# Strips of 64 bytes between the tiles of x, and one tile less for inner results, in a fused attention and expert kernel

## The chip, the core and the metric

The kernel runs on one core of a Trainium2 chip. The metric is the device time of one execution in microseconds (us). The time before is the median of 2 runs; the profile is of one more execution.

## The reference

Three stages follow each other. N is 2,304 tokens, D is 512.

```python
# 1 attention with keys and values averaged over 8 positions
k_p, v_p = k.reshape(B, H, 72, 8, 64).mean(3), v.reshape(B, H, 72, 8, 64).mean(3)
x = softmax(q @ k_p.T / 8) @ v_p                # 4 x 8 heads, 576 queries, 64 wide
x = x.transpose(0, 2, 1, 3).reshape(2304, 512)
# 2 a dense layer
h = x @ w_in                                    # 512 -> 2048
x = (h * cos(h)) @ w_out                        # 2048 -> 512
# 3 eight experts, weighed by a gate that is normalized eight times over rows and columns
P = exp(x @ w_gate - max); 8 times: P /= rowsum; P /= colsum; P *= N / E
out = sum over e of P[:, e] * (relu(x @ w1[e]) @ w2[e])   # 512 -> 1024 -> 512
```

## The kernel before, in words

**Arithmetic.** Every large product is made from numbers that are split into a high and a low part (float32r). Of the four partial products three are made: high by high, high by low, low by high. So each block of 128 by 128 weights costs three matmuls.

**Experts.** An expert's 1,024 inner columns are cut into two units of 512, so there are 16 units. The tokens are cut into three pairs of blocks, each block 384 tokens wide. A *step* is one unit with one pair; there are 48. A step has a first layer and a second layer, both in a scheme of seven products (P1, P5, P6, P2, P7, P3, P4, in this order) instead of eight. The first layer (`first_layer`, matmuls at L1178) makes the seven products for each half h of the unit: 2 x 7 products of 6 matmuls, 384 columns each, 84 in all. Its moving operand is a tile of x (`xc`), its weights are `whi` and `wlo`. It writes the PSUM tiles px, py and pv. ACT and DVE turn the results into 14 pairs of inner tiles `gh`, `gl`. The second layer (`strassen_layer`, matmuls at L1563) takes them as weights and streams `vhi` and `vlo`, 256 columns each, into the PSUM tiles pc and qc: 126 matmuls a step. While one step's second layer runs, the first layer of the next step runs between its parts.

**Tiles in SBUF.** The pool `xp` has eight tiles of 6,144 bytes a partition. In the attention and the dense layer they are x itself (`xh`, `xl`) and other things; in the experts seven of them hold the seven forms of x, one fixed tile for each product, and the eighth is `spare`, which DVE and ACT use. Each of the seven is filled again by a DMA from DRAM (`x_loaded`, issued by SP) for every step. Right behind the pool `xp` lies the pool `wp`: 14 tiles of 2,048 bytes for `whi` and `wlo`. 6,144 is three times 2,048, so before the change all these tiles start at the same remainder modulo 2,048 bytes (704). Within a tile the kernel reads pieces that start at multiples of 512 bytes. The inner tiles are 1,536 bytes; their pools hold 6 + 12 for `gh` and 6 + 12 for `gl` (GB = 12).

**Order.** Nothing is issued in the order of the Python code. Every operation becomes a node of a graph with an engine and a duration that the code states. `Graph.schedule` simulates five engines, and takes again and again the operation that can start first (of those near it the one with the earliest due time). It gives out the tiles too: an operation whose kind has no free tile can't be taken. This makes the order that each engine has on the chip. Where the simulated PE would idle by over 0.5 us it puts in filler matmuls (`keep_busy`, L529). The order of the pool tiles in memory is that in which they are first used: xh1, xh2, xl1, xl3, xl2, xh3, xh0, xl0.

Of the kernel before, what the change touches and what calls it, by code (L numbers as in the profile page):

```python
# [10 lines left out]
F32 = mybir.dt.float32  # L11
# [12 lines left out]
P = 128  # L24
# [41 lines left out]
class Slot:  # L66

    def __init__(self, group, pool, tag):
        self.group, self.pool, self.tag, self.free, self.holder, self.kinds = group, pool, tag, 0.0, None, []


class Group:

    def __init__(self, graph, name, side, after=(), over=None):
        self.graph, self.name, self.side, self.after, self.over = graph, name, side, after, over
        self.kinds, self.pools, self.stack, self.users, self.closed = [], {}, None, 0, False

    def ready(self):
        return self.stack is not None or (
            all(g.users == 0 for g in self.after) and (self.over is None or self.over.ready()))  # L80
# [72 lines left out]
class Graph:  # L153
# [119 lines left out]
    def schedule(self, log=None):  # L273
# [28 lines left out]
        while left:  # L302
# [38 lines left out]
            for buf in node.bufs:  # L341
                kind = buf.kind
                if not kind or buf.slot:
                    continue
                kind.queue.remove(buf)
                slot = slots.pop(0)
                slot.group.open()
                slot.holder, buf.slot = buf, slot
                buf.tile = slot.group.pools[slot.pool].tile(buf.shape, buf.dtype, tag=f"{slot.pool}{slot.tag}", name=buf.name)
            gap = start - free[e] + (0.6 if 19.0 < start < 27.0 else 0.0)  # L350
            if e == "PE" and self.fill and gap > 0.5:
                room = last and last.spare and all(
# [96 lines left out]
def fused_kernel(ctx: ExitStack, tc: tile.TileContext, qT, kT, kS, vS, v0, k1, v1, wa1, wb1, wa2, wb2, wg, out):  # L449
    nc = tc.nc  # L450
    g = Graph(ctx, tc)
    add, buf = g.add, g.buf

    W1, W2, GB, XR, T5 = 14, 14, 12, 7, 2
    base = g.group("base")
    first = g.group("first")
# [6 lines left out]
    more = g.group("more", "left", (second,))  # L463
# [6 lines left out]
    def many(group, pool_name, n, strict=False):  # L470
        return g.kind(group, pool_name, [str(i) for i in range(n)], strict)
# [30 lines left out]
    k_s5, k_c22, k_t5 = many(late, "cps", 2), many(late, "cpc", 1), many(late, "cpt", T5)  # L502
    k_acc2 = {2 * pair + j: k for pair, ks in ((1, [many(more, f"acx{n}", 1, True) for n in range(2)]), (0, k_acc[2:]),
                                               (2, k_acc[:2])) for j, k in enumerate(ks)}
    k_gbh, k_gbl = (g.join(many(first, a, 6), many(more, b, GB), strict=3) for a, b in (("gph", "gbh"), ("gpl", "gbl")))

    def banks(*names, strict=False):
        return g.kind(psum, "ps", [str(n) for n in names], strict)
# [1186 lines left out]
```

## Time and profile before

| | us |
|---|---|
| median of 2 runs | 1903.39 (1903.32 to 1903.47) |
| profiled execution | 1907.59 |
| its span, first to last instruction | 1905.9 |
| PE busy in it | 1889.6 (99%) |
| DVE, ACT, POOL busy | 1504.0, 1102.6, 360.7 |
| last 48 steps (experts), from first to last matmul | about 500 to 1901 of the span |

The profiled execution is 4.2 us (0.2%) above the median of the runs. PE is the matmul engine; its weight loads have a row of their own, PEld. A matmul's own duration overlaps the next one, since matmuls are pipelined. What a matmul costs is therefore the distance from its start to the next start; the chain of waits shows it, because it counts each stretch once.

### The profile page before, as it was taken

To read this page: it belongs to the slowest core of one execution; us is meant where nothing else is said; L and a number is where in the kernel's file an instruction comes from. 1 tells how busy PE (TensorE), PEld (TensorE's weight loads), DVE (VectorE), ACT (ScalarE), POOL (GpSimd) and SP (SyncE) were. 2 spreads that over 40 slices of the span, in tenths; PEclk is the share of its full clock that TensorE was granted. 3 is DMA by queue.
4 is the path that set the end of the run, shared out by engine and by line. 5 is a ranking of instruction groups with operands and counts; after the bars stand their busy time and mean duration, and the time that the engine had idled before them with its cause. 6 is when DMAs were issued, how large, how long until landed. Compare 5 with 4: busy or idle time off the path is not lost.

```text
span 1905.9 us, 33965 instructions
## 1 busy us (share of the span) xinstructions
PE 1889.6 (99%) x13032; PEld 1853.0 (97%) x13032; DVE 1504.0 (79%) x2721; ACT 1102.6 (58%) x2375; POOL 360.7 (19%) x260
## 2 busy tenths in 40 slices
PE   9999999999999999999999999999999999999999
PEld 7789998899999999999999999999999999999998
DVE  7998856987787787778787787877877877878776
ACT  5865434675566665555555565555555565655653
POOL 0213332242102021212122121212121120212120
PEclk9999999999999999999999999999999999999999
DMA  8856662577656556556456465565465564655653
GB/s 267 245 187 238 239 169 71 188 256 263 232 224 254 202 202 262 187 210 243 185 208 257 155 250 212 191 261 198 196 243 194 199 265 160 244 221 191 235 217 116
DMA packets 104762, 406.76 MB, mean 213 GB/s; under 512 B 11160, under 2 KB 15896, under 8 KB 102552
## 3 DMA queue, kind: packets, MB, share of 16 engines
q1 hardware_dynamic: 102616, 400.01, 56.2%
q0 software_dynamic: 1984, 4.59, 1.4%
q8 instruction: 102, 1.67, 0.3%
q14 instruction: 60, 0.49, 0.1%
HBM read 363.40 MB, written 41.16 MB: 212 GB/s over the span
## 4 chain that ended last, share of the span: by engine, by line
PE 93%; DVE 4%; ACT 2%; DMA 1%; issue 0%; SPq 0%; ACTq 0%; DVEq 0%
PE pc L1563 20%; PE py L1178 17%; PE qc L1563 16%; PE px L1178 11%; PE pv L1178 11%; PE po L989 3%; PE po L990 3%; PE po L991 3%; PE ph L989 2%; PE ph L990 2%; PE ph L991 2%; PE px L897 1%; PE ptr L883 0%; DMA wc<-wac 0%; DVE xd L557 0%
## 5 line engine op out<-in xcount | busy, mean ns | idle before, releaser
L1563 PE MATMUL pc<-vlo,gh 128*128 128x256 f32 x1152 | 318.0, 276 | 0.0
L1563 PE MATMUL pc<-vhi,gl 128*128 128x256 f32 x1152 | 318.0, 276 | 0.0
L1563 PE MATMUL pc<-vhi,gh 128*128 128x256 f32 x1152 | 318.0, 276 | 0.0
L1178 PE MATMUL py<-xc,whi 128*128 128x384 f32 x1152 | 293.7, 335 | 0.0
L557 DVE TENSOR_TENSOR gl<-sf,gh 128x384 fp32r<-128x384 f32 x384 | 228.4, 624 | 29.4 <-ACT gh L540 29.2
L540 ACT ACTIVATE gh<-sf 128x384 fp32r<-128x384 f32 x384 | 194.8, 524 | 93.6 <-DVE sf L557 91.5
L1563 PE MATMUL qc<-vhi,gh 128*128 128x256 f32 x864 | 241.7, 280 | 0.9 <-DVE qc L557 0.5
L1563 PE MATMUL qc<-vlo,gh 128*128 128x256 f32 x864 | 239.0, 277 | 0.0
L1563 PE MATMUL qc<-vhi,gl 128*128 128x256 f32 x864 | 238.9, 276 | 0.0
L557 POOL TENSOR_TENSOR raw<-raw 128x512 f32<-128x512 f32 x46 | 60.1, 1307 | 930.3 <-DVE wlo L557 584.4
L1563 PEld LDWEIGHTS pc<-vhi,gh 128*128 128x128 f32 x1152 | 216.3, 188 | 0.1
L1563 PEld LDWEIGHTS pc<-vhi,gl 128*128 128x128 f32 x1152 | 216.3, 188 | 0.0
L1563 PEld LDWEIGHTS pc<-vlo,gh 128*128 128x128 f32 x1152 | 216.2, 188 | 0.0
L1178 PEld LDWEIGHTS py<-xc,whi 128*128 128x128 f32 x1152 | 199.3, 188 | 0.9 <-ACT py L540 0.6
L1178 PE MATMUL px<-xc,whi 128*128 128x384 f32 x768 | 196.5, 336 | 0.0
L1178 PE MATMUL pv<-xc,whi 128*128 128x384 f32 x768 | 196.1, 336 | 0.0
L1178 PE MATMUL py<-xc,wlo 128*128 128x384 f32 x576 | 192.5, 334 | 0.0
L1563 PEld LDWEIGHTS qc<-vhi,gh 128*128 128x128 f32 x864 | 162.1, 188 | 4.6 <-DVE qc L557 0.9
L1563 PEld LDWEIGHTS qc<-vhi,gl 128*128 128x128 f32 x864 | 162.4, 188 | 0.0
L1563 PEld LDWEIGHTS qc<-vlo,gh 128*128 128x128 f32 x864 | 162.1, 188 | 0.0
L1178 PEld LDWEIGHTS px<-xc,whi 128*128 128x128 f32 x768 | 130.1, 188 | 0.6 <-issue 0.6
L1178 PEld LDWEIGHTS pv<-xc,whi 128*128 128x128 f32 x768 | 130.3, 188 | 0.0
(245 smaller groups left out, 4578.6 us busy)
## 6 DMA issues: line engine op xcount, KB each, us to landing
xc<-xc SPq DMA_DIRECT2D x357, 768.0 KB, 6.7
wc<-wac SPq DMA_DIRECT2D x112, 256.0 KB, 4.6
raw<-wb SPq DMA_DIRECT2D x32, 512.0 KB, 7.8
raw<-wa SPq DMA_DIRECT2D x32, 512.0 KB, 4.7
raw<-wa SPq DMA_DIRECT2D x8, 1024.0 KB, 7.2
raw<-wb SPq DMA_DIRECT2D x8, 1024.0 KB, 6.2
wac<-m SPq DMA_DIRECT2D x12, 512.0 KB, 6.3
wac<-cw SPq DMA_DIRECT2D x12, 512.0 KB, 3.7
```

The costliest lines, as they stand in the source:

```text
L540: lambda: nc.scalar.activation(out=out(), in_=in_(), func=func, **{k: v() if callable(v) else v for k, v in more.items()}),
L557: (nc.gpsimd if e == "G" else nc.vector).tensor_tensor(out=out(), in0=in0(), in1=in1(), op=op)
L897: nc.tensor.matmul(out=bank[e * D:(e + 1) * D, off:off + n], lhsT=vs[b][:, 2 * hp + e, :], rhs=pt[:, 2 * hh + e, off:off + n], start=(off ...
L989: nc.tensor.matmul(out=ps, lhsT=lh, rhs=rh, start=(i == 0), stop=False)
L990: nc.tensor.matmul(out=ps, lhsT=lh, rhs=rl, start=False, stop=False)
L991: nc.tensor.matmul(out=ps, lhsT=ll, rhs=rh, start=False, stop=(i == total - 1))
L1178: nc.tensor.matmul(out=ps(), lhsT=l[:, k], rhs=r[:, c, :], start=(start and c + n == 0), stop=(c + n == 3), skip_group_check=True)
L1563: nc.tensor.matmul(out=ps, lhsT=l[:, r], rhs=m[:, k], start=(start and h + n == 0), stop=(h + n == 3), skip_group_check=True)
```

## The change

Three things are done. A strip of 64 bytes is taken from the pool `xp` before each of its tiles, in order of first use, but not before the fourth (`spare`'s neighbour); one more strip follows the eighth. That is eight strips, 512 bytes. To have room, the second part of the pool for `gl` has 11 tiles instead of 12.

```diff
         self.kinds, self.pools, self.stack, self.users, self.closed = [], {}, None, 0, False
+        self.seen = []
...
                 slot.holder, buf.slot = buf, slot
+                if slot.pool == "xp" and slot not in slot.group.seen:
+                    slot.group.seen.append(slot)
+                    n = len(slot.group.seen)
+                    if n != 4:
+                        slot.group.pools[slot.pool].tile([P, 16], F32, tag=f"xpgap{n}", name="gap")
                 buf.tile = slot.group.pools[slot.pool].tile(buf.shape, buf.dtype, ...)
+                if slot.pool == "xp" and len(slot.group.seen) == 8:
+                    slot.group.seen.append(None)
+                    slot.group.pools[slot.pool].tile([P, 16], F32, tag="xpgap9", name="gap")
...
-    k_gbh, k_gbl = (g.join(many(first, a, 6), many(more, b, GB), strict=3) for a, b in (("gph", "gbh"), ("gpl", "gbl")))
+    k_gbh, k_gbl = (g.join(many(first, a, 6), many(more, b, n), strict=3) for a, b, n in (("gph", "gbh", GB), ("gpl", "gbl", GB - 1)))
```

Where the tiles start, as the two programs lay them out (remainder modulo 2,048 bytes):

| tile (product in the experts) | before | after | x minus weights, modulo 512, before | after |
|---|---|---|---|---|
| xh1 (P7) | 704 | 768 | 0 | 64 |
| xh2 (P1) | 704 | 832 | 0 | 128 |
| xl1 (P2) | 704 | 896 | 0 | 192 |
| xl3 (`spare`) | 704 | 896 | 0 | 192 |
| xl2 (P3) | 704 | 960 | 0 | 256 |
| xh3 (P4) | 704 | 1024 | 0 | 320 |
| xh0 (P5) | 704 | 1088 | 0 | 384 |
| xl0 (P6) | 704 | 1152 | 0 | 448 |
| weights `whi`, `wlo` | 704 | 1216 | | |

The second layer's tiles keep their distances: `gh` and `gl` start at 448 modulo 512 before and after, `vhi` and `vlo` at 128, so the moving operand minus the weights is 192 in both.

The instruction counts stay, but for two filler matmuls. PE's order is the same up to the first expert unit; from there a few places of it move, since the pool of `gl` is smaller. In the steady state it repeats every three steps; one of three is as before.

The first place is the 25th step on PE. py is P6 of the first half, px is P2; pc is the second layer. Before:

```order
L1178 MATMUL py<-xc,whi 128x384 x2
L1178 MATMUL py<-xc,wlo 128x384
L1178 MATMUL py<-xc,whi 128x384 x2
L1178 MATMUL py<-xc,wlo 128x384
L1563 MATMUL pc<-vhi,gh 128x256
L1563 MATMUL pc<-vlo,gh 128x256
L1563 MATMUL pc<-vhi,gl 128x256
```

Changed (the lines stand nine further down):

```order
L1187 MATMUL py<-xc,whi 128x384 x2
L1187 MATMUL py<-xc,wlo 128x384
L1187 MATMUL py<-xc,whi 128x384 x2
L1187 MATMUL py<-xc,wlo 128x384
L1187 MATMUL px_14292<-xc,whi 128x384 x2
L1187 MATMUL px_14292<-xc,wlo 128x384
L1187 MATMUL px_14292<-xc,whi 128x384 x2
L1187 MATMUL px_14292<-xc,wlo 128x384
L1572 MATMUL pc<-vhi,gh 128x256
```

P2 moved ahead of 12 matmuls of the second layer. This is so in one of three steps.

The second place is SP's queue in the same stretch; xc is a tile of x, raw a tile for weights of the second layer (wb) or the first (wa). Before:

```order
L562 DMA raw_13175<-wb 128x1024
L562 DMA xc<-xc 128x1536
L562 DMA raw_13199<-wb 128x1024
L562 DMA raw<-wa 128x1024
L562 DMA xc<-xc 128x1536 x7
```

Changed:

```order
L571 DMA xc<-xc 128x1536 x14
L571 DMA raw_13191<-wb 128x1024
L571 DMA raw_13205<-wb 128x1024
L571 DMA raw<-wa 128x1024
L571 DMA xc<-xc 128x1536 x7
```

The first load of wb now stands behind a load of x that was behind it.

The third place is PE at the end of the last step's first layer, where py is P4 of the second half. Changed:

```order
L1187 MATMUL py<-xc,whi 128x384 x2
L1187 MATMUL py<-xc,wlo 128x384
L1187 MATMUL py<-xc,whi 128x384 x2
L1187 MATMUL py<-xc,wlo 128x384
L538 MATMUL pc<-ident 128x128 x2
```

The last row, two filler matmuls, is new.

## Rows read from the trace of the kernel before

**Rows 1.** The page: engines, busy us, share of the span, instructions.
```profile
PE 1889.6 (99%) x13032; PEld 1853.0 (97%) x13032; DVE 1504.0 (79%) x2721; ACT 1102.6 (58%) x2375; POOL 360.7 (19%) x260
```

**Rows 2.** Windows: stretch, length, each engine's busy us, granted clock, DMA share.
```profile
600.00:1880.00 1280.00, 1280.00 (x9265) 1277.01 (x9265) 1003.26 (x1832) 735.34 (x1634) 222.09 (x159) 1.00 0.56 215
```

**Rows 3.** Chain of waits, 600 to 1880: shares of the stretch by line.
```profile
by line: PE pc L1563 28.2%; PE py L1178 21.6%; PE qc L1563 21.4%; PE px L1178 14.5%; PE pv L1178 14.4%
```

**Rows 4.** Windows of one line alone, L1178 then L1563 (PE, PEld busy and counts).
```profile
600.00:1880.00 1280.00, 710.28 (x3709) 627.58 (x3709) 1.00 0.56 215
...
600.00:1880.00 1280.00, 698.84 (x5556) 684.50 (x5556) 1.00 0.56 215
```

**Rows 5.** Chain of waits, 918 to 947, in order: start, us, what.
```profile
919.08 1.05 PE py L1178 x6
920.12 1.36 PE pc L1563 x12
921.49 1.04 PE px L1178 x6
922.53 1.04 PE py L1178 x6
923.57 0.68 PE qc L1563 x6
...
924.93 1.05 PE pv L1178 x6
```

**Rows 6.** Chain of waits, 420 to 445 (the dense layer).
```profile
422.03 1.04 PE pv L1178 x6
423.07 1.04 PE py L1178 x6
424.12 0.18 PE po L989
...
424.66 1.04 PE px L1178 x6
425.70 1.04 PE pv L1178 x6
```

**Rows 7.** Timeline, weight loads then matmuls: start, us, engine, line, operation.
```profile
602.58 0.36 PEld L1178 LDWEIGHTS px<-xc,whi 128*128 128x128 f32 x2
...
602.58 0.33 PE L1178 MATMUL px<-xc,wlo 128*128 128x384 f32 x1
```

**Rows 8.** Timeline: a `gl` tile is written, an older one's last read, its first read.
```profile
1237.53 0.55 DVE L557 TENSOR_TENSOR gl<-spare,gh 128x384 fp32r<-128x384 f32 x1
...
1239.43 0.28 PE L1563 MATMUL pc<-vhi,gl 128*128 128x256 f32 x1
...
1252.28 0.28 PE L1563 MATMUL pc<-vhi,gl 128*128 128x256 f32 x1
```

**Rows 9.** Timeline of SP, then the matmul that reads the first of these tiles.
```profile
1183.83 3.77 SPq L562 DMA_DIRECT2D xc<-xc  x3
1187.65 0.57 SPq L562 DMA_DIRECT2D raw<-wb  x1
1189.69 0.32 SPq L562 DMA_DIRECT2D xc<-xc  x1
1190.85 0.33 SPq L562 DMA_DIRECT2D raw<-wb  x1
...
1194.66 0.52 PE L1178 MATMUL px<-xc,whi 128*128 128x384 f32 x2
```

**Rows 10.** Loads of x, 600 to 1880, issue to landing.
```profile
DMA to landing us min/median/max: 4.0/6.8/9.2
```

**Rows 11.** Timeline of ACT: the first read of a loaded wb tile.
```profile
1212.24 0.64 ACT L540 ACTIVATE vhi<-raw 128x512 fp32r<-128x512 f32 x1
```

**Rows 12.** Filler matmuls of L529 by tile: count, duration ns min/median/max.
```profile
L529 PE MATMUL px<-ident x10: 275/275/377, 25.0 to 27.1; 128*128 128x128 f32 x10
```

## The prediction

> **What bounds the kernel now.** I began with the shares of the engines: PE is busy for 99% of the span [rows 1]. Then the windows, since an average hides stages: in the experts, from 600 to 1880 us, PE is busy in all 1280.00 us at a granted clock of 1.00, while DVE has 277 us to spare (1003 of 1280), ACT 545 and POOL over 1000 [rows 2]. The granted clock of 1.00 is the upper of the two levels, 2.4 GHz. So in two thirds of the kernel nothing counts but what a matmul costs and whether PE is made to wait.
>
> What a matmul costs is read from the chain of waits, stretch by stretch [rows 5]: six matmuls of the first layer take 1.04 us, so 173.3 ns each; twelve of the second take 1.36 us, six 0.68, so 113.3 ns. Now the average: the first layer's three tiles have 14.5 + 21.6 + 14.4 = 50.5% of the stretch [rows 3], which is 646.4 us for 3709 matmuls [rows 4], 174.3 ns each. The second layer's 49.6% are 634.9 us for 5556, 114.3 ns each. Both layers stand 1 ns above their floor. In the whole stretch that is 3.6 us in the first layer and 5.4 us in the second. All waits and all disturbance of PE are in these 9 us; the reader should keep this number, since a change that only takes disturbance away can't give more.
>
> **The strips.** They move the moving operand of the first layer against its weights. Do the two disturb each other at distance 0? They are read at the same time: the load of the next weights starts with the matmul, both at 602.58 [rows 7]. But the rows show no harm in it. First, the floor is reached at distance 0: px and py at 921.49 and 922.53 take 1.04 us [rows 5], and there all pieces are a multiple of 512 bytes apart. Second, in the dense layer the products of the same kind take the same 1.04 us [rows 6]; the four in these rows stream other tiles of x past other weights, by the layout at 64, 64, 256 and 320. The second layer of the experts, at 192, keeps to one floor throughout, too. Third, the excess shows where it comes from: a product takes 1.05 us where it follows the second layer (py at 919.08, pv at 924.93) and 1.04 where it follows another product. It is a change from 256 to 384 columns, some 0.01 us each, not a matter of seven tiles that all lie alike. Something like it stands in the dense layer, where three matmuls of po take 0.18 instead of 0.17 each behind py [rows 6].
>
> So the bounds of the strips are: a gain of 3.6 x 4032 / 3709 = 3.9 us if all excess of the first layer were a clash, and a loss from distances that no row shows. Of the seven, 64, 192, 256, 320 and 448 have been seen (448 in the last matmul of the second layer, while `whi` is loaded); 128 and 384 haven't. Those are P1 and P5: 2 products x 2 halves x 6 matmuls x 48 steps = 1152. The worst that a row shows for one matmul of this width beside its floor is 0.18 against 0.1733, 6.7 ns: 1152 x 6.7 ns = 7.7 us. I take 0, the value of five distances out of seven.
>
> The Trainium skill, page "SBUF — State Buffer", section "Who interferes with whom", gives PE two independent read ports, one for the moving operand and one for the weights, and says that PE never waits on anyone. By that rule the strips are worth exactly 0; the trace agrees as far as it goes.
>
> `spare` moves too, and the tiles of x in the dense layer. DVE and ACT have the slack named above, and in the dense layer PE could win no more than the same nanosecond for each of some 1,100 matmuls, so I put both at 0.
>
> **One tile less for `gl`.** A step needs 14; there were 18, now there are 17. What is hit is a `gl` that is written while 17 others are held. In the experts that is one of 14 writes in a step; reckoned buffer by buffer it is always one that is early. The example: DVE writes it at 1237.53; the oldest of the others is last read at 1239.43 and so is free at 1239.71; PE first reads the new one at 1252.28 [rows 8]. Written 2.2 us later it would still be 12 us early. The other two kinds of step have 3.1 and 6.2 us to wait with 15 and 18 us of room. So the tile itself costs 0; what can cost is the order that follows from it.
>
> **The order on PE.** In two of three steps a few products move by two to five groups of six matmuls of the second layer. The number of changes from second to first layer stays (424 before, 422 after), so that excess stays too. I counted the distance on PE between each product and the next that needs its result, with 1.04 us a product and 0.68 a group. The tightest of each kind stays as it was: P1 to P6 1.72 us, P6 to P7 2.40, P4 to the next P6 2.76. One shrinks, P7 to P4 of the first half, from 5.12 to 3.76 us; but 3.76 is what the second half has in every step, without a wait. Cost 0.
>
> P2 of the first half moves 1.36 us ahead in one step of three, and its tile is loaded again for each step. The load is issued at 1183.83, the matmul starts at 1194.66 [rows 9]: 10.83 us, the least that any of the seven has. Loads of x take 6.8 us, 9.2 at most [rows 10]. With 1.36 us less there are 9.47 us: still above 9.2. Cost 0, with the thinnest cover of all that I found.
>
> **SP's queue.** The first wb load moves behind a load of x that waits for PE: from 1187.65 to behind 1189.69, some 2.4 us. Its first reader is at 1212.24 [rows 11], 24 us after the old issue. Cost 0.
>
> **The end.** Two filler matmuls before the last stretch of the second layer. Each stands in the trace as two records; with 275 ns as the duration of one [rows 12] 4 x 0.275 = 1.1 us is the upper bound, and since durations overlap I take half, 0.5 us. The planner puts them where it saw PE wait anyway.
>
> **The sum.** 0 + 0 + 0 + 0.5: the profiled execution would take 1908 instead of 1907.59. It stands 4.2 us above the median of the runs; against the median that makes 1903.9, so 1904. About 2% (38 us) is what a measurement of this kernel can tell from no change, and this is far inside.
>
> **Rivals.**
> 1. *The excess is a clash and the strips end it.* Against it: the three points above. For it: all tiles lay at distance 0 wherever 1.05 stands, so no row shows the same change of width at another distance. 1903.4 - 3.9 = 1899.5. Chance 0.15.
> 2. *The floor itself is a clash.* 384 columns at 2.4 GHz are 160 ns; the rows show 13.3 ns more. If the strips gave that back: 4032 x 13.3 = 54 us, 1850 us. Against it: the same floor at distances 64, 256 and 320, and a surplus that grows with the columns (6.7 ns at 256, 13.3 at 384) while the weight load beside it stays the same. Chance 0.01. The Trainium skill, page "TensorE: Matmul & The Clock Gate", section "Back-to-back issue gap", gives N / 2.4 + 2.5 ns; by that formula 384 columns cost 162.5 ns, and 4032 x 10.8 = 44 us would be open. The trace disagrees with it at every distance it has.
> 3. *The load for P2 comes too late (slower).* This decides from 9.47 us on. 16 steps have the earlier P2. If their loads land as late as the worst seen, 9.2, nothing happens; two wb loads of 512 KB that now follow each other could add a microsecond or two: 16 x 1.5 = 24 us, 1927. For 2% each of the 16 would have to be 2.4 us late. With rows of 6.8 us in the median: chance 0.06, of that 0.01 for over 2%.
> 4. *The unseen distances 128 and 384 clash.* 1903.4 + 7.7 = 1911. Chance 0.04.
> 5. *The change doesn't do what it says.* The layout does show the seven distances, so this is left at 0.
>
> The forecast, no change by more than 2 us: 0.74.
>
> **Range and chances.** Down to 1898, which holds rival 1 and a little for the dense layer; up to 1910, which holds most of rival 4 and the smaller outcomes of rival 3. Left out are the floor, late loads in earnest, and an offset between runs. Faster by over 2%: 0.01 (rival 2). Slower by over 2%: 0.01 (rival 3). Within: 0.98.
>
> **What would show it.** In the changed profile: px, py and pv still near 50.5% of the stretch from 600 to 1880. If 1.05 becomes 1.04 for products behind the second layer, rival 1 holds. If one product of P1 or P5 takes more than 1.05 while P7 doesn't, rival 4. Idle time of PE before px at L1187 that ends with a DMA is rival 3. The forecast is wrong if PE's busy share of the experts falls under 99%, or if the floors of 1.04 and 0.68 us move at all.

## The result, and the profile after

The changed kernel takes 1927.37 us (median of two runs, 1924.46 and 1930.27), the one before 1903.39. The ratio is 1.0122 (1.0102 to 1.0143). It is 24 us slower, where 1904 was forecast, with 1910 as the upper end.

First the page of the changed kernel, the line that answers to [rows 1].

```profile
PE 1907.7 (99%) x13036; PEld 1869.8 (97%) x13036; DVE 1502.6 (78%) x2723; ACT 1096.9 (57%) x2374; POOL 367.3 (19%) x259
```

PE's busy time has grown by 18.1 us with four matmul records more, while DVE, ACT and POOL stand within 7 us of where they stood. So PE does the same work more slowly. The same windows as in [rows 2] and [rows 4], first all engines, then the first layer's line alone, then the second layer's:

```profile
600.00:1880.00 1280.00, 1277.03 (x9141) 1272.57 (x9140) 988.55 (x1811) 724.66 (x1620) 231.43 (x160) 1.00 0.57 213
...
600.00:1880.00 1280.00, 705.52 (x3654) 618.85 (x3655) 1.00 0.57 213
...
600.00:1880.00 1280.00, 698.61 (x5487) 687.02 (x5485) 1.00 0.57 213
```

The granted clock is 1.00 as before (the upper level, 2.4 GHz), and yet PE gets through 9141 matmuls in these 1280 us instead of 9265: 1.3% fewer. For 3.0 us it isn't busy at all; before it always was. The busy time by line doesn't show which matmuls are slower, since matmuls overlap. The chain of waits does. The stretch that answers to [rows 5], in the 14th step (start, us, what):

```profile
918.53 0.68 PE qc L1572 x6
919.21 0.68 PE pc L1572 x6
919.89 0.68 PE qc L1572 x6
920.57 0.68 PE pc L1572 x6
921.25 1.05 PE py L1187 x6
922.30 0.71 PE qc L1572 x6
923.01 0.71 PE pc L1572 x6
923.72 0.71 PE qc L1572 x6
924.42 1.05 PE px L1187 x6
925.48 1.06 PE pv L1187 x6
926.54 0.69 PE qc L1572 x6
927.23 1.04 PE py L1187 x6
928.27 1.36 PE pc L1572 x12
929.63 1.04 PE px L1187 x6
930.68 1.05 PE py L1187 x6
931.72 0.71 PE qc L1572 x6
932.43 0.71 PE pc L1572 x6
933.14 1.04 PE pv L1187 x6
934.18 0.68 PE qc L1572 x6
```

This is the main finding, and it is to be read from top to bottom. In this stretch pv at 925.48 is P5 and px at 924.42 is P1. Six matmuls of the second layer take 0.68 us, four times in a row. Then one product of the first layer runs (py, P4, whose x now lies at 320 from the weights), and from then on the same six take 0.71, three times in a row. Behind P1 and P5 (128 and 384) it is 0.69, all but the fast form. P6 (py at 927.23, distance 448) is followed by the fast form (1.36 for twelve), P2 and P7 (929.63, 930.68; 192 and 64) by the slow one, P3 (933.14; 256) by the fast one again. The second layer's own tiles haven't moved against each other. It has two speeds; it changes from one to the other at products of the first layer, and then it mostly stays for the whole stretch.

Over all steps, worked out from every matmul's start in the trace, gaps of over 30 ns left out: the second layer's mean distance from start to start is 113.52 ns before and 115.77 after. Of its stretches from 600 us on, 5% were slow (above 115.8 ns) before and 49% are after. P3 is always followed by a fast stretch (89 of 89), P4 and P1 together always by a slow one (58 of 58). But the last product and its distance don't decide alone: P4 by itself is followed by a slow stretch in 23 of 30 cases, P5 and P6 together in 14 of 14 behind a fast stretch and in none of 31 behind a slow one. So what ran before counts as well.

The second piece is the idle time of PE. The list of waits of the changed kernel (600 to 1880 us; before, it was empty):

```profile
PE py L1187 <- DVE pv L566: 3.0, 14, 0.2
```

With this most of the 24 us are divided. In the profiled executions the experts last from the first matmul's start to the last's 1402.8 us before and 1421.7 after: +18.9. Second layer: 6,048 matmuls x 2.25 ns = 13.6 us. First layer: 4,032 x 0.48 ns (174.27 to 174.75) = 1.9 us. The gaps of over 30 ns: 6.6 to 9.7, so 3.1 us. That makes 18.6. The experts also begin 3.8 us later (498.6 to 502.4); in ten kernels with the old order on every engine they begin between 491.0 and 501.3, so I don't put this down to the change. The matmuls into `po` ahead of the experts, some 1,100, cost 173.82 ns before and 174.04 after, which is 0.2 us in all.

### The profile page after: what moved, and what is told of

The parts are those of the page before. It is cut to its first block, busy times and chain, and to the rows that moved or that the text cites. A ratio compares the mean times of both kernels' runs of the same rounds, so it can differ in the third digit from the quotient of the medians.

```text
span 1928.5 us, 33987 instructions
## 1 busy us (share of the span) xinstructions
PE 1907.7 (99%) x13036; PEld 1869.8 (97%) x13036; DVE 1502.6 (78%) x2723; ACT 1096.9 (57%) x2374; POOL 367.3 (19%) x259
## 4 chain that ended last, share of the span: by engine, by line
PE 85%; DVE 9%; DMA 2%; ACT 2%; issue 1%; SPq 0%; POOL 0%; DVEq 0%; POOLq 0%; ACTq 0%
PE pc L1572 19%; PE py L1187 15%; PE qc L1572 15%; PE pv L1187 10%; PE px L1187 9%; PE po L998 3%; PE po L999 3%; PE po L1000 3%; DVE gl L566 2%; PE ph L998 2%; PE ph L1000 2%; PE ph L999 2%; DVE sf L566 1%; DMA wsum<-wac 1%; DVE acc L1559 1%
## 5 line engine op out<-in xcount | busy, mean ns | idle before, releaser
L566 DVE TENSOR_TENSOR gl<-sf,gh 128x384 fp32r<-128x384 f32 x384 | 207.4, 569 | 31.4 <-ACT gh L549 31.3
```

Of the source, the lines that this page charges most:

```text
L566: (nc.gpsimd if e == "G" else nc.vector).tensor_tensor(out=out(), in0=in0(), in1=in1(), op=op)
```

## The experiments

Two theories stood at the start. **D**: the distance between the first layer's moving tile and its weights makes the loss. **O**: the moved order does. Later D was split into **X** (x minus the first layer's weights alone decides) and **G** (the places of all four groups of tiles against each other).

The table holds all kernels. W1 are the first layer's weights (`whi`, `wlo`), W2 the second's (`gh`, `gl`), v its moving tiles (`vhi`, `vlo`). The distances are in bytes modulo 256; that 256 is the period is shown below. "Second" and "first" are the mean ns from start to start, "experts" is from their first matmul to the last, in us. All three are of the profiled execution. The ratio is that of the runs, against the kernel before beside them.

| kernel | x-W1 | v-W2 | x-W2 | v-W1 | second | first | experts | ratio |
|---|---|---|---|---|---|---|---|---|
| before | 0 | 192 | 0 | 192 | 113.52 | 174.27 | 1402.8 | 1 |
| after | mixed | 192 | mixed | 192 | 115.77 | 174.75 | 1421.7 | 1.0122 |
| e1 | 0 | 192 | 0 | 192 | 113.47 | 174.27 | 1406.4 | 1.0011 |
| e4 (256) | 0 | 192 | 0 | 192 | 113.39 | 174.19 | 1405.4 | 1.0020 |
| e2 (64) | 64 | 192 | 64 | 192 | 117.81 | 173.43 | 1423.1 | 1.0111 |
| e3 (64) | 64 | 192 | 64 | 192 | 117.67 | 173.41 | 1426.8 | 1.0125 |
| e7 (320) | 64 | 192 | 64 | 192 | 117.70 | 173.41 | 1426.9 | one run |
| e5 (128) | 128 | 192 | 128 | 192 | 115.32 | 176.45 | 1424.6 | one run |
| e8 (384) | 128 | 192 | 128 | 192 | 115.30 | 176.44 | 1424.4 | one run |
| e6 (192) | 192 | 192 | 192 | 192 | 114.90 | 173.99 | 1413.3 | one run |
| e11 (32) | 32 | 192 | 32 | 192 | 115.09 | 173.40 | 1408.1 | 1.0041 |
| e9 | 192 | 192 | 0 | 128 | 118.09 | 173.56 | 1425.2 | 1.0136 |
| e10 | 224 | 192 | 0 | 160 | 117.76 | 174.89 | 1428.6 | 1.0150 |
| f1 | 0 | 192 | 64 | 128 | 115.85 | 175.89 | 1422.7 | 1.0124 |
| e12 | 0 | 224 | 0 | 224 | 118.20 | 174.72 | 1430.5 | 1.0150 |
| f2 | 0 | 0 | 0 | 0 | 119.10 | 174.10 | 1433.3 | 1.0158 |
| f3 | 0 | 64 | 0 | 64 | 117.54 | 174.64 | 1426.1 | 1.0128 |
| f5 | 0 | 128 | 0 | 128 | 118.94 | 175.28 | 1437.1 | 1.0194 |
| f4 | 64 | 0 | 64 | 0 | 119.41 | 173.51 | 1432.8 | 1.0162 |

### Distance or order

e1 is the changed kernel without the strips; the tile less for `gl` and the order that follows from it stay.

```diff
-                    if n != 4:
-                        slot.group.pools[slot.pool].tile([P, 16], F32, tag=f"xpgap{n}", name="gap")
...
-                    slot.group.pools[slot.pool].tile([P, 16], F32, tag="xpgap9", name="gap")
```

> The smaller gl pool alone, without strips: every engine's order is that of the changed kernel, the tiles of x are at distance 0 as before. Theory D (the distance puts PE into a state in which each matmul is some 4.5 ns slower, and the new order only adds the wait for pv): second-layer matmuls at 113 ns again (bad stretches under 5%), the wait of 0.49 us in one step of three stays, 14 x 0.49 = 7 us, so about 1910 us. Theory O (the new order does all of it, the distance nothing): 1924 to 1930 us, with the 118 ns stretches.

Measured: 1906.32 us, ratio 1.0011 (0.9999 to 1.0022). The order alone is worth about 2 us in the runs, which is not clear of noise, and 3.6 in the experts of the profile. What it is shows in the waits of e1:

```profile
PE py L1178 <- DVE pv L557: 3.4, 14, 0.3
```

It is the same wait as in the changed kernel, 14 times, and no strip is there.

e2 is the reverse: the kernel before with its order on all engines. The weights' pool is laid ahead of x and one strip of 64 bytes between them. 64 bytes less in a table (`sel`) keep every tile behind that table where it was; the four tiles of sums (`acc`) and a gate table, which lie in between, move by 64 bytes too.

```diff
+                if slot.pool == "xp" and not slot.group.seen:
+                    slot.group.seen.append(slot)
+                    slot.group.pools[slot.pool].tile([P, 16], F32, tag="xpgap", name="gap")
...
+    k_w1 = many(base, "wp", W1, True)
...
-    k_w1 = many(base, "wp", W1, True)
...
-        ("ones", [P, P]), ("wgr", [P, KC, GW]), ("sel", [P, 6 * E]), ("lg", [P, NT, E]), ("pr", [P, NT, E]))}
+        ("ones", [P, P]), ("wgr", [P, KC, GW]), ("sel", [P, 4 * E]), ("lg", [P, NT, E]), ("pr", [P, NT, E]))}
```

> The order of the kernel before on every engine (18 gl tiles), but all eight tiles of x stand 64 bytes modulo 512 from the weights (the weights' pool is laid first, one strip between the pools, a gate table 64 bytes smaller so that all later tiles stay where they were). Theory D: distance 64 left the slow state behind it in the changed kernel every time, so nearly all of the second layer is slow: 6048 x 4.5 ns = 27 us, and some in the dense layer, 1925 to 1940 us, without any wait for pv. Theory O: 1903 us.

Measured: 1924.66 us, ratio 1.0111 (1.0085 to 1.0136). Without any moved instruction nearly the whole loss is there. The chain of waits of e2 over 600 to 1880 us, its pieces from 919 us on, and the windows of the second layer's line:

```profile
by line: PE pc L1567 28.8%; PE qc L1567 21.7%; PE py L1182 21.2%; PE px L1182 14.2%; PE pv L1182 14.1%
...
919.24 1.04 PE px L1182 x6
920.28 1.04 PE pv L1182 x6
921.32 0.70 PE qc L1567 x6
922.03 1.04 PE py L1182 x6
923.07 1.41 PE pc L1567 x12
```

```profile
600.00:1880.00 1280.00, 709.15 (x5469) 694.72 (x5468) 1.00 0.55 213
```

50.5% of 1280 us for 5469 matmuls are 118.2 ns, against 114.3 from [rows 3, 4]. And py at 922.03, a product behind the second layer (qc at 921.32), takes 1.04 us, not the 1.05 of [rows 5]: at 64 the first layer loses its excess, 174.27 to 173.43 ns. So the gain of the prediction's rival 1 exists, 4,032 x 0.84 = 3.4 us. The second layer takes back more than seven times that: 6,048 x 4.29 = 25.9 us.

### Which distances, and their period

e3 to e8 are the changed kernel with its order, but with the strips gathered: one of d bytes ahead of all tiles of x and one of 512 - d behind them, so all seven have one distance. The edit for d = 64, the others by the two numbers:

```diff
-                    if n != 4:
-                        slot.group.pools[slot.pool].tile([P, 16], F32, tag=f"xpgap{n}", name="gap")
+                    if len(slot.group.seen) == 1:
+                        slot.group.pools[slot.pool].tile([P, 16], F32, tag="xpgap1", name="gap")
...
-                    slot.group.pools[slot.pool].tile([P, 16], F32, tag="xpgap9", name="gap")
+                    slot.group.pools[slot.pool].tile([P, 112], F32, tag="xpgap9", name="gap")
```

e3, all at 64:

> The changed kernel with its eight strips gathered into two, 64 bytes ahead of the tiles of x and 448 behind them: all seven at distance 64, the order as in the changed kernel. Theory D: all of the second layer slow plus the wait for pv, 1903 + 27 + 7 = 1937 us. Theory O: as the changed kernel, 1927 us.

Measured: 1928.15 us, ratio 1.0125 (1.0106 to 1.0144).

e4, all at 256:

> As e3, but 256 bytes ahead and 256 behind: all seven at distance 256, where P3 of the changed kernel always ended the slow state. Theory D: no slow stretches, only the wait for pv, as e1, about 1910 us. Theory O: as the changed kernel, 1927 us.

Measured: 1906.48 us, ratio 1.0020 (1.0008 to 1.0033). The loss is gone with all 512 bytes of strips in place; what is left is the order's part, the same wait as in e1 (3.2 us, 14 times).

e5 to e8, one run each, at 128, 192, 320 and 384:

> All seven tiles of x at distance 128 (the order of the changed kernel, 512 bytes of strips in all). Theory D, as the changed kernel showed P1 at this distance (slow behind it in 60 of 74 cases): mostly slow, some 4.4 ns a second-layer matmul, 24 us above e1. A rival, that only distance 64 is bad and the others were dragged along by it: as e1.

> All seven at 192. In the changed kernel the stretch behind P2 alone, at this distance, was slow in 13 of 13 cases, but the one before it had been slow too. Theory D: slow, 24 us above e1. Rival (P2 only kept a state that another product had set): as e1.

> All seven at 320. In the changed kernel P4, at this distance, was followed by a slow stretch in 23 of 30 cases where a fast one had gone before. Theory D: slow in most of the second layer, 15 to 24 us above e1. Rival (P4 comes ahead of P1 and something else is late there): as e1.

> All seven at 384. In the changed kernel P5, at this distance, was followed by fast second-layer matmuls in 14 of 14 cases. Theory D: fast, as e1. Since P5 was itself dear (17 to 26 ns a product above its floor), up to 5 us more in the first layer.

Measured: 1929.02, 1918.76, 1931.33 and 1927.9 us, beside one run of the kernel before at 1910.0. The profiles settle more than these single times: 64 and 320 agree to 0.03 ns in the second layer, 128 and 384 to 0.02, 0 and 256 to 0.1. Where x moves against all else, only the remainder modulo 256 bytes counts. The first layer loses most at 128 (176.45 ns), the second at 64. The chain of e5, from 921 us on:

```profile
921.37 1.06 PE px L1186 x6
922.43 1.05 PE pv L1186 x6
923.49 0.71 PE qc L1571 x6
```

In e5 all seven products have one distance, and still the second layer changes its speed. From 600 us on, a single product is followed by a fast stretch in all 191 cases, two in a row by a slow one in 142 of 195, three by a slow one in 13 of 13. So the number of products between two stretches counts too, not only the distance.

### Moving the weights, or the second layer, instead of x

The next four keep the old order on every engine. e9 moves the weights by 64 bytes (a strip behind the last tile of x), so that x stands at 448, which is 192 modulo 256; e10 by 32; e11 is e2 with a strip of 32 bytes. In all three `sel` is smaller by as much, and `acc` moves with the strip, as in e2. The strip of e9:

```diff
+                if slot.pool == "xp" and len(slot.group.seen) == 8:
+                    slot.group.seen.append(None)
+                    slot.group.pools[slot.pool].tile([P, 16], F32, tag="xpgap", name="gap")
```

> The kernel before in its own order on every engine; one 64-byte strip between the last tile of x and the weights, so x minus weights is 448 for all seven. The order's part is taken out. Theory D (distance, with a period of 256 bytes, so that 448 acts as 192): second layer as with all seven at 192, about 114.9 ns, first layer about 174.0 ns; without the order's wait the time is 1908 to 1913. If the period were not 256 bytes, 448 could be anything from 1903 (as 0) to 1925 (as 64). Rival O (the order alone makes the loss): 1903.

Measured: 1930.15 us, ratio 1.0136 (1.0121 to 1.0151), second layer 118.09 ns. This contradicts what I had expected from D: by x minus weights, e9 is e6, and e6 has 114.90 ns. x minus the first layer's weights doesn't decide alone.

> The kernel before in its own order; a 32-byte strip between the last tile of x and the weights: x minus weights is 480, so 224 modulo 256, which no run has had. Theory D gives a time between its neighbours 0 (1903.5) and 192 (about 1911): 1903 to 1911, a second layer of 113.4 to 115 ns. If the 1 ns that the first layer loses behind the second goes away here without the slow second layer, up to 3 us less: 1900. Rival O: 1903.

Measured: 1932.14 us, ratio 1.0150 (1.0135 to 1.0165), 117.76 ns; not between its neighbours either.

> The kernel before in its own order; the weights lie ahead of x and a 32-byte strip between them: x minus weights is 32 for all seven. Theory D gives a time between its neighbours 0 (1903.5) and 64 (1924.7). If the distance acts in pieces of 64 bytes, 32 is one of its two neighbours and not between them: the second layer is at 113.4 or at 117.8 ns. Rival O: 1903.

Measured: 1911.26 us, ratio 1.0041 (1.0027 to 1.0056), 115.09 ns. So 32 bytes do count, and the second layer is at neither of the two values: 42% of its stretches are slow, up to 19 in a row, and the pattern mostly repeats every 54 stretches. In e6, 27 slow ones follow 27 fast ones or more, four times over; from 1409 us on most are fast. The speed can outlast many changes of layer.

e12 leaves x and weights alone and takes out the two edges of 32 bytes, of which one lies ahead of the second layer's moving tiles. That moves these by 32, and with them the other tiles on that side, inner tiles of DVE among them.

```diff
-        if self.name in ("early", "mid"):
-            edge = self.stack.enter_context(self.graph.tc.tile_pool(name="edge" + self.name, bufs=1, side=self.side))
-            edge.tile([P, 8], F32, name="edge" + self.name)
```

> The kernel before in its own order with x minus weights 0; the two 32-byte edges on the other side of memory are left out, so the second layer's moving tiles stand at 224 instead of 192 from its weights, modulo 256. Theory D as read so far (the first layer's distance sets how fast the second layer's stretch behind it runs, its own distance doesn't): second layer 113.5 ns, time 1903. If the second layer's own distance counts too: anything up to 117.8 ns and 1925, or below 113.3 ns and down to 1900.

Measured: 1933.36 us, ratio 1.0150 (1.0135 to 1.0165), 118.20 ns. The place of the second layer's moving tiles counts as well, and at once as much as the whole change.

### Which of the four distances

f1 has the strip of 64 bytes ahead of x and weights together (e2's edit without the moved pool), so x minus W1 stays 0 and v minus W2 192. Only the distances across the change of layer are new.

> The kernel before in its own order; one 64-byte strip ahead of x and weights together. x minus weights stays 0, as before; only x against the second layer's weights (64 instead of 0) and the second layer's moving tiles against the first layer's weights (128 instead of 192, modulo 256) change. Theory X (x minus weights sets the state of the second layer): 113.5 ns, 1903 to 1906. Theory G (the places of all four groups of tiles against each other set it, also across the change of layer): second layer above 115 ns, 1915 to 1930.

Measured: 1926.44 us, ratio 1.0124 (1.0106 to 1.0142). X falls: neither layer's own distance has changed, and 53% of the second layer's stretches are slow.

f2, f3 and f5 change the edge alone to 224, 160 and 96 bytes, f4 joins e2 with the edge of 224. The edit of f2:

```diff
-            edge.tile([P, 8], F32, name="edge" + self.name)
+            edge.tile([P, 56 if self.name == "mid" else 8], F32, name="edge" + self.name)
```

> The kernel before in its own order; the edge beside the second layer's moving tiles is 224 bytes instead of 32, so that these stand at 0 from their own weights and, as x does, at 0 from the first layer's weights, modulo 256: all four distances are 0. Theory X: 1903. Theory G: not known in advance, 1900 (if the product behind the second layer loses its 9 ns as well) to 1930.

> The kernel before in its own order; the same edge at 160 bytes: the second layer's moving tiles stand at 64 from both kinds of weights, x at 0. Theory X: 1903. Theory G: 1903 to 1930.

> The kernel before in its own order with x at 64 from the weights (which alone made the second layer 117.8 ns and the time 1924.7), and the edge at 224 bytes, so that the second layer's moving tiles stand at 0 from both kinds of weights. Theory X: 117.8 ns and 1925 again. Theory G: the harm of 64 can go away, down to 1900, or stay.

> The kernel before in its own order; the edge beside the second layer's moving tiles at 96 bytes instead of 32: they stand at 128 from both kinds of weights, modulo 256, x at 0. Theory G (the places of all tiles against each other decide, the second layer's own among them): no number follows from the others; between the best seen at x 0 (192: 113.5 ns, 1903) and the worst (0: 119.1 ns, 1933). If 192 is not special and 128 is as good, 1900 to 1906; if 192 is the only good place of the four, 1924 to 1933. Theory X (x minus weights alone): 1903.

Measured: 1933.18 us (ratio 1.0158, 1.0137 to 1.0179), 1928.65 (1.0128, 1.0108 to 1.0147), 1934.14 (1.0162, 1.0143 to 1.0180) and 1940.42 (1.0194, 1.0177 to 1.0211). The chain of f2, all four distances 0, from 921 us on, and the windows of f2 (all engines):

```profile
921.02 1.43 PE pc L1563 x12
922.45 1.04 PE px L1178 x6
923.49 1.04 PE py L1178 x6
924.53 0.71 PE qc L1563 x6
925.24 0.72 PE pc L1563 x6
```

```profile
600.00:1880.00 1280.00, 1280.00 (x9067) 1279.01 (x9066) 992.55 (x1803) 725.39 (x1605) 216.11 (x158) 1.00 0.55 211
```

1.43 us for twelve is slower than the slow form of e2 (1.41), and there is no idle time: 9067 matmuls instead of 9265. With f4 the other hope falls too: the harmful 64 isn't cured by another place of the second layer. G holds in the sense that each of the groups that was moved mattered. Of the layouts tried, only that of before and its copies at 256 keep the second layer at 113.5 ns, and no version beats the kernel before.

One rival has to be named: no run moves PE's operands alone. In e3 and e5 to e8, set against e4, only the pool of x moves, but `spare`, which DVE and ACT use, lies in it. In e9 `spare` stays and `acc` moves with the weights; in f2, f3 and f5 only tiles on the other side of memory move, among them DVE's. So no tile of another engine moves in all of these runs, and PE's operands do in each. That makes them the likeliest cause; a run that moves them by themselves is lacking.

## Why the prediction was wrong

**"The strips": this step failed, with its price of 0.** Its first two points are true of the first layer at the distances that they name: the floor of 173.3 ns does hold at 64, e2 shows it better than any row I had. What failed is the inference from it. I looked for the harm in the matmuls whose operand moves. Most of it falls on those behind them, in a layer whose tiles don't move against each other. My bounds, +7.7 and -3.9 us, were both worked out for matmuls of the first layer, 1,152 and all 4,032; the 6,048 of the second stood in neither. The sentence "the second layer of the experts, at 192, keeps to one floor throughout, too" took a fact of one layout for a property of that distance: in the same trace 5% of the stretches already were slow, and at the same 192 e2 has 117.81 ns.

The rows of the dense layer [rows 6] could not have shown it: from 420 to 445 us all its matmuls have 384 columns. How a matmul's start stands to the start of its own weight load tells the layers apart. In the changed kernel's second layer a matmul starts 110 ns after that in a fast stretch (918.4 to 920.9 us) and 114 to 115 in a slow one (922.1 to 923.1), and the next weight load starts 2 to 4 ns later. These two make the whole 113.3 or 117.7. In the first layer it is 170 to 172 ns. So it may be that the second layer goes as fast as a weight load beside a running matmul, and that the first has some 55 ns to spare per matmul, which would hide a load that is 4 ns longer. This is argued, not shown. The recorded durations don't single out the load: in the second layer of e2 a load is recorded with 188.8 ns (187.4 before), a matmul with 281.3 (276.7 before). And it doesn't say why the first layer loses 2.2 ns at 128 in spite of that room. That the moving operand of the second layer is what is slower stays a rival.

The rule that I cited, the Trainium skill's page "SBUF — State Buffer", section "Who interferes with whom" (two independent read ports, PE never waits on anyone), is contradicted by e3 against e4 if the cause lies in SBUF: with the same instructions in the same order the place of the pool of x alone makes the second layer 4.3 ns a matmul slower (117.67 and 113.39). Its result that the strips are worth exactly 0 was in agreement with my rows only because these came from the first layer and the dense layer at 0, 64, 256 and 320, where the first layer loses little or nothing (173.4 to 174.3 ns).

**"The order on PE": cost 0 failed by some 3 us.** I counted the distances on PE alone, and these held: all 14 waits are at a P7 that stands behind P6 as it did before, with twelve matmuls of the second layer and P2 between, 2.40 us. What was late is DVE, whose order, and POOL's, I did not count. The changed kernel's DVE, POOL and PE around the place (start, us, engine, line, operation):

```profile
1231.89 2.14 DVE L566 TENSOR_TENSOR gl<-spare,gh 128x384 fp32r<-128x384 f32 x2
...
1235.07 1.66 DVE L566 TENSOR_TENSOR sf<-sf 128x384 f32<-128x384 f32 x1
1236.66 0.55 DVE L566 TENSOR_TENSOR pv<-py,s 128x384 f32<-128x384 f32 x1
...
1234.73 1.59 POOL L566 TENSOR_TENSOR vlo<-raw,vhi 128x512 fp32r<-128x512 f32 x1 [1.59 <-ACT vhi L549]
...
1237.27 0.62 PE L1187 MATMUL py<-xc,whi 128*128 128x384 f32 x2 [0.22 <-DVE pv L566]
```

P7 needs the PSUM tile that `pv<-py,s` empties. In DVE's queue it stands behind `sf<-sf`, which takes 1.66 us here. The same place before:

```profile
1219.64 1.66 DVE L557 TENSOR_TENSOR gl<-spare,gh 128x384 fp32r<-128x384 f32 x1
...
1222.36 1.00 DVE L557 TENSOR_TENSOR sf<-sf 128x384 f32<-128x384 f32 x1
1223.29 0.55 DVE L557 TENSOR_TENSOR pv<-py,s 128x384 f32<-128x384 f32 x1
...
1221.39 1.56 POOL L557 TENSOR_TENSOR vlo<-raw,vhi 128x512 fp32r<-128x512 f32 x1 [0.50 <-PE pv L1178]
...
1224.61 0.51 PE L1178 MATMUL py<-xc,whi 128*128 128x384 f32 x2
```

There it ended at 1223.84, 0.77 us ahead of P7. Two things in DVE's queue take that away. Two `gl<-spare` stand in front now instead of one (2.14 us against 1.66), and `sf<-sf` meets more of a POOL operation. It takes 0.55 us where none runs beside it (82 of 96 cases before); behind a `vlo` that POOL is at work on it ends 0.41 us after that, at 1223.36 before and at 1236.73 now, and the `vlo` started 0.34 us ahead of it now, 0.97 before. Together that is 0.48 and 0.66 us, 1.1 in all. P2, which moved, has no part in these 14 places. e1 (1.0011), e4 (1.0020) and e3 against e2 (1928.15 and 1924.66 us, the same distances in the two orders) each put the order at 2 to 4 us.

**One tile less for `gl`, SP's queue, the P2 load: right.** e1 has no wait but the one above, and no wait for a DMA stands in the list of the changed kernel. The loads of x there answer to [rows 10]:

```profile
DMA to landing us min/median/max: 4.0/6.1/8.7
```

So rival 3 did not happen. **The fillers:** four records of `pc<-ident` stand at 1907.5 to 1907.8 us, within the 1.1 us that bounded them.

**The rivals.** Rival 1's mechanism is real at 64 and 32 (173.4 ns), and lost in what came with it. Rival 2 is out: the lowest mean of the first layer in any kernel is 173.40 ns. The formula that I set beside it is given by the Trainium skill, page "TensorE: Matmul & The Clock Gate", section "Back-to-back issue gap", for a single matmul by itself, so the rows, a stream with a weight load for every matmul, don't speak against it. Rival 4 had the right sign, and at 128 and 384 the first layer does lose 2.2 ns a matmul (e5, e8), against the 6.7 that I took as the worst; but in the changed kernel all of the first layer comes to 1.9 us. P5, at 384, does take 1.06 us there (pv at 925.48), yet P7, at 64, rises as much on average (P5 by 2.0 ns a matmul, P7 by 2.1), so it isn't a matter of the two unseen distances. It had the wrong layer as well. The last sentence of the prediction named the true sign: the floor of 0.68 us moved, to 0.71. I had given it no mechanism and no chance, and so the range had no room for it. The 2% that I took as the least that a measurement can tell was wrong, too: the interval here is 1.0102 to 1.0143, so 1.2% is told clearly.

## What to carry to other kernels

Where matmuls with different operands follow each other, the price of a layout can be paid by matmuls whose operands did not move: at 64 all of it fell on the second layer, at 128 on both. So bound the loss with the count of every kind of matmul in the stream. A floor that one trace shows everywhere is the floor of that one layout. And when an order changes, follow the queue of the engine that empties a PSUM tile, not only the distances on PE.

## What the runs showed of the hardware

- The second layer (256 columns, 128 x 128 float32r weights) has at its own distance of 192 two main speeds, 113.3 and 117.7 ns a matmul. It stays in one for whole stretches, in e6 for 27 in a row, and changes over, but for few places, at products of the first layer.
- Moving x by 256 bytes changes nothing, by 64 or 320 the same (117.7 ns in both), by 128 or 384 the same (115.3, a mean of fast and slow stretches). Even 32 bytes count (e11, e12).
- At other own distances the means are others: 117.5 ns at 64, 118.9 at 128, 119.1 at 0, 118.2 at 224, with x at 0.
- A DVE operation of 128x384 with both inputs in SBUF (`sf<-sf`) takes 0.55 us by itself and 1.66 or 1.00 beside a running POOL operation; in both it ends 0.41 us after that one.
- Why the period is 256 bytes, and what inside PE or SBUF keeps the speed, stays open: no run here looks inside. Whether v against its own weights or v against the first layer's counts in e12, f2, f3 and f5 isn't separated, since both moved together.
